# New tables of queue offsets for a fused attention and maxout kernel: own tables on both sides of a batch border, one operand turned by DMA there, casts of the first groups in load order

## The chip, the cores and the metric

One core of a Trainium2 chip. The metric is the device time of one execution in microseconds; times of several executions are given as the median. Each execution also has a span, the time from the first to the last instruction that the profile shows, mostly 1.8 us shorter than the timed figure (1.7 to 3.8 on record), and a mean granted TensorE clock (1.000 is full speed). All executions quoted are in the fast state. The engines are called PE (TensorE), DVE (VectorE), ACT (ScalarE), POOL (GpSimd) and SP (the engine that issues the DMAs).

## The reference, cut to what matters

```python
# q, k, v: (4, 12544, 128)   agents: (4, 49, 128)   w1, w2, w3: (128, 768)   w_out: (768, 128), all float32
def sm(a, b):
    s = scale * (a @ b.transpose(0, 2, 1))
    e = np.exp(s - s.max(-1, keepdims=True))
    return e / (e.sum(-1, keepdims=True) + 1e-09)
agent_v = sm(agents, k) @ v              # (4, 49, 128): needs all of k and v of a batch
x = (sm(q, agents) @ agent_v).reshape(B * S, D)
h = np.maximum(np.maximum(x @ w1, x @ w2), x @ w3)
return h @ w_out
```

Everything for q of batch b waits for the sums over all k and v of batch b. The kernel therefore reads k and v of batch b+1 while it works on q of batch b. A **batch border** is the place where the sums of the next batch are finished and q goes over to it.

## The kernel before

q is worked in 49 groups of 8 tiles of 128 rows (98 tiles a batch, so a border falls inside a group). For each group there are q scores and their exponential, six first-half products `u0..u5`, six relus of them (`a0..a5`, one in place), six second-half products `v0..v5`, six maxima (`x0..x5`, one of them a relu on ACT), 26 output matmuls for each of two output tiles, and two scalings. The instructions are not written in program order: each has an offset, and all are sorted by six units times the group plus the offset. The order of the sorted list is the order of each engine's queue; an instruction that waits at the head of a queue holds up what stands behind it, as the waits of 0.60 and 0.96 us in the prediction's timelines show.

```python
KEY = {"qt": -5.826, "qe": -4.714, "s": -3.397, "ex": -3.144, "ho": -2.653, ...}   # groups with k and v beside them
LATE = {"oc04": -102.316, "s": -5.143, "ex": -3.890, "ho": -3.007, ...}            # groups of the last batch
PRODUCT_KEYS = (-6.500, -6.260)
...
for op in sorted(ops, key=lambda o: o[:2]):     # in emit(): go, or wait for what it needs, or for a free tile
    if not go(op): late.append(op) ...
...
rings = {"uv": (3, []), "om": (2, []), "a": (3, [])}   # hidden tiles, small tiles, relu buffers
```

The work at a border is `k_tail`. A reduction on DVE sums the exponentials of k, a matmul with ones (the total) adds them over the partitions, a reciprocal and a multiplication give the normalised `avT`, and two products of it with the weights, evacuated by ACT, give the table `G` that the hidden products of the next batch use.

```python
def reduce():    nc.vector.tensor_reduce(out=d["e"], in_=Eacc[b]..., op=ALU.add)          # L328
def total():     nc.tensor.matmul(host[s][:, :A], ones, d["e"], ...)                      # L333
def normalise(): nc.vector.reciprocal(r, r) ; nc.vector.tensor_tensor(avT, Vacc, r, mult) # L339, L342
def product():   nc.tensor.matmul(...) ; nc.scalar.activation(G[b][:, c0:c1], src, Copy)  # L354, L361
...
elif s < SB:                                     # q of all groups but those of the last batch
    put("qt", turn_q, ring="om", frees=[("qe", s)])           # 8 PE transposes, L417
    put("qe", evacuate, ("qt", s), ...)                       # copy by DVE, L422
else:                                            # last batch
    at(key + K["s"] - 5.5, turn_q_dma, ("qe", s))             # DMA transpose
```

The softmax here doesn't subtract the row's maximum and nothing guards it: scores larger than these inputs give would overflow.

Of the kernel before, what the change touches and what calls it, by code (L numbers as in the profile page):

```python
# [16 lines left out]
def kernel(  # L17
# [32 lines left out]
    SB = (B - 1) * NT // GT  # L50
    assert NT % 2 == 0 and B * NT % GT == 0


    KEY = {
        "qt": -5.826, "qe": -4.714, "s": -3.397, "ex": -3.144, "ho": -2.653, "ks": -2.585,
        "ke": -1.395, "u0": -1.385, "u1": -0.945, "a0": -0.578, "a1": -0.505, "kv": -0.272,
        "sum": -0.189, "rec": -0.160, "ka": -0.096, "v0": -0.088, "u3": 0.041, "a3": 0.349,
        "x0": 0.448, "v1": 1.119, "v3": 1.156, "x1": 1.388, "u2": 1.556, "x3": 2.207, "u4": 2.461,
        "a2": 2.461, "v2": 2.540, "a4": 2.626, "x2": 2.904, "u5": 3.056, "v4": 3.065, "a5": 3.309,
        "x4": 3.802, "v5": 4.472, "x5": 5.223, "lin0": 6.482, "oc02": 6.840, "oc03": 7.560,  # L60
        "oc04": 8.286, "oc00": 8.460, "oc01": 8.460, "oc05": 8.461, "sc0": 8.860, "lin1": 9.007,
        "oc15": 9.269, "oc10": 9.504, "oc12": 9.761, "oc11": 11.129, "oc13": 11.301,
        "oc14": 11.651, "sc1": 11.652,
    }
    LATE = {
        "oc04": -102.316, "s": -5.143, "ex": -3.890, "ho": -3.007, "u0": -2.479, "sum": -2.401,
        "a0": -2.109, "u1": -1.115, "rec": -0.632, "u2": -0.631, "a1": -0.201, "v1": -0.150,
        "u3": 0.004, "a2": 0.202, "a3": 1.295, "x1": 1.296, "v0": 1.603, "v3": 1.692, "x0": 1.773,
        "v2": 1.787, "x3": 2.014, "x2": 2.121, "u4": 2.761, "u5": 2.826, "a4": 2.857, "v4": 3.484,
        "a5": 3.667, "v5": 3.891, "x4": 4.081, "x5": 4.963, "lin1": 6.405, "oc14": 6.642,  # L70
        "oc12": 6.780, "oc10": 8.128, "oc11": 8.220, "oc15": 8.227, "oc13": 8.498, "sc1": 8.670,
        "lin0": 9.304, "oc01": 9.553, "oc00": 9.686, "oc03": 11.369, "oc02": 11.426,
        "oc05": 11.684, "sc0": 12.804,
    }
    PRODUCT_KEYS = (-6.500, -6.260)

    const = ctx.enter_context(tc.tile_pool(name="const", bufs=1))
    loads = ctx.enter_context(tc.tile_pool(name="loads", bufs=14))
# [131 lines left out]
    def k_group(b, t0, n, key, s):  # L210

        d = {}
        early = s is None

        def load():
            for name, src in (("k", k), ("v", v)):
# [72 lines left out]
        if early:  # L289
            g = ("early", t0)  # L290
            at(key - 30, load)
            at(key - 5, cast_k)
            at(key - 4, cast_v)
            at(key, turn_k, ("kt", g), (), "uv", [("kt_out", g)])
            at(key + 0.5, evacuate, ("kt_out", g), [("kt", g)])

            last = [("normalise", 0)] if t0 + n == NT else []
            late = max(0, (key - last_key) / 6 + 2)
            at(min(key + 6.6, last_key + 0.58 + 0.02 * late), scores, ("ks", g), [("kt_out", g)],
               "uv", [("ka", g)] + last)  # L300
            at(min(key + 7, last_key + 0.64 + 0.01 * late), exps, ("ke", g), [("ks", g)])
            done = last_key + (0.6 + 0.1 * late if late >= 1 else 0.55)
            at(min(key + 13.2, done), values, ("kv", g), [("ke", g)])
            at(min(key + 13.6, done + 0.01), add_values, ("ka", g), [("kv", g)])
        else:
            at(key + KEY["ks"] - 22, load)
            at(max(key + KEY["ks"] - 10, last_key - 3.4), cast_k)
            at(max(key + KEY["ks"] - 8, last_key - 3.3), cast_v)
            if s > 1:
                at(max(key + KEY["ks"] - 6.5, last_key - 3.2), turn_k, ("kt_out", s))  # L310
            else:

                turn = 1.2 if s else last_key + 1.05
                at(turn, turn_k, ("kt", s), (), "uv", [("kt_out", s)])
                at(turn + 0.05, evacuate, ("kt_out", s), [("kt", s)])

            at(key + KEY["ks"] if s else KEY["u0"] + 0.6, scores, ("ks", s), [("kt_out", s), ("ho", s)])
            at(key + KEY["ke"], exps, ("ke", s), [("ks", s)])
            at(key + KEY["ke"] + 1.5, add_exps, ("kx", s), [("ke", s)])
            at(key + KEY["kv"], values, ("kv", s), [("ke", s)])  # L320
            at(key + KEY["ka"], add_values, ("ka", s), [("kv", s)])

    def k_tail(b, sum_key, keys, s):
        d = {}
# [60 lines left out]
    def q_group(s):  # L385
# [33 lines left out]
        def evacuate():  # L419
# [3 lines left out]
            else:  # L423
                nc.scalar.activation(d["qT"].rearrange("p j c -> p (j c)"), d["qT_ps"], AF.Copy)

        def turn_q_dma():
            d["qT"] = work.tile([P, GT, P], BF16, tag="qT", bufs=3, name="qT")
            nc.sync.dma_start_transpose(out=d["qT"], in_=d["qb"].rearrange("p j c -> p (j c)"))
# [83 lines left out]
            for src, r0, r1, m in rows(d["out"]):  # L512
                nc.sync.dma_start(out[r0:r1, :].rearrange("(p j) c -> p j c", j=m), src)

        K = KEY if s < SB else LATE
        new = [("product", tails[s], i) for i in range(2)] if s in tails else []

        def put(name, fn, *needs, ring=None, frees=()):
# [4 lines left out]
        if s == 0:  # L523
            at(last_key - 29.9, load)
            at(last_key - 3.5, cast)
            at(last_key + 0.82, turn_q, ("qt", 0), (), "om", [("qe", 0)])
            at(last_key + 0.825, evacuate, ("qe", 0), [("qt", 0)])
            at(last_key + 1, scores, ("s", 0), [("qe", 0)], "om", [("ex", 0)])
            at(last_key + 1.01, exps, ("ex", 0), [("s", 0)])
        elif s < SB:  # L530
            at(key + K["qt"] - 20, load)
            at(max(key + K["qt"] - 7, last_key - 3), cast)
            put("qt", turn_q, ring="om", frees=[("qe", s)])
            put("qe", evacuate, ("qt", s), *([("s", s - 3)] if s >= 3 else []))
        else:
            at(key + K["s"] - 24, load)
            at(key + K["s"] - 8, cast)
            at(key + K["s"] - 5.5, turn_q_dma, ("qe", s))
        if s:
            put("s", scores, ("qe", s), ring="om", frees=[("ex", s)])  # L540
            put("ex", exps, ("s", s), *old)
# [1 line left out]
        if s:  # L543
            put("ho", host_tile, ring="om", frees=[("rec", s)] + extra)
        else:
            at(KEY["u0"] - 0.04, host_tile, ("ho", 0), (), "om", [("rec", 0)] + extra)
        put("sum", sums, ("ex", s), ("ho", s),
            *([("ks", s)] if s in hosting else [("total", s)] if s + 1 in tails else []))
        put("rec", recips, ("sum", s))
# [12 lines left out]
        for o in range(2):  # L562
            put(f"lin{o}", lambda o=o: out_linear(o), ("ex", s), *new, ring="om", frees=[(f"sc{o}", s)])
            for f in range(NF):
                put(f"oc{o}{f}", lambda o=o, f=f: out_hidden(o, f), (f"lin{o}", s), (f"x{f}", s))
            put(f"sc{o}", lambda o=o: out_scale(o), ("rec", s),
                *[(f"oc{o}{f}", s) for f in range(NF)], *([("store", s - 3)] if s >= 3 else []))
        at(key + max(K["sc0"], K["sc1"]) + 0.5, store, ("store", s), [("sc0", s), ("sc1", s)])

    def ramp():  # L570

# [27 lines left out]
        if 4 <= g < len(first_sizes) - 5:  # L599
            fillers += [(first_key + 6.0 * g + 0.55, 3), (first_key + 6.0 * g + 1.3, 3)]  # L600
    k_tail(0, last_key, (last_key + 0.95, last_key + 1.02), None)
    for key, n in fillers + [(last_key + 0.9, 2), (last_key + 1.1, 2)]:
        at(key, lambda n=n: keep_busy(n), ("busy", key), (), "om", [("busy", key)])
    tails = {b * NT // GT: b for b in range(1, B)}
    hosting = set()
    for b in range(1, B):
        for g in range(NK):
# [2 lines left out]
            k_group(b, g * KT, min(KT, NT - g * KT), 6.0 * s, s)  # L610
    for s, b in tails.items():
        assert s - 1 not in hosting
        k_tail(b, 6.0 * (s - 1) + KEY["ho"] + 0.001, [6.0 * s + PRODUCT_KEYS[i] for i in range(2)], s - 1)
    for s in range(NQ):
        q_group(s)
    ramp()
# [33 lines left out]
```

## Time and profile before

| | |
|---|---|
| time | 470.73 us, median of 3 (470.11 to 471.0) |
| span of the profiled execution | 467.5 us, clock 0.998 |
| PE, DVE, ACT busy | 94%, 87%, 85% |
| ordinary group / group ahead of a border / late group | 8.35 / 10.85 / 7.84 us |

Four groups of the page's costliest instructions carry the argument. The columns are line, engine, operation, output and input, count, then busy us and mean ns of one, then the idle time ahead of them and what ended most of it.

```profile
L485 DVE TENSOR_TENSOR r<-uv_ps,a_sb 128x1024 bf16<-128x1024 f32 x245 | 297.3, 1220 | 13.9 <-PE uv_ps L460 4.2
L475 ACT ACTIVATE a_sb<-uv_ps 128x1024 bf16<-128x1024 f32 x245 | 241.3, 1028 | 11.5 <-PE uv_ps L460 11.1
L460 PE MATMUL uv_ps<-e_q,G 49*128 49x512 bf16 (+3 forms) x1248 | 185.5, 368 | 4.8 <-DVE r L485 2.9
...
L490 PE MATMUL o_ps<-G,e_q 128*128 128x256 bf16 x196 | 38.0, 276 | 1.8 <-DVE o_sb L506 1.8
```

L485 is the maximum, L475 the relu, L460 the hidden products, L490 the first matmuls of an output tile and L506 the scaling that frees one. PE waited 4.8 us ahead of hidden products and 1.8 us ahead of output tiles in the whole run. A group of L460 or L485 mixes all stages, so the stages are read from windows and timelines.

In all that follows the row-sum matmuls of a group are its marker. "c10 to c14" is the time from those of group 10 to those of group 14, counted from 0: the four groups around the first border.

### The profile page before, as it was taken

The numbers are of one execution on the slowest core, as the hardware profiler recorded it, in microseconds if no ns is written. First come the engines' busy times: TensorE is split into PE (matmuls) and PEld (weight loads), VectorE is DVE, ScalarE is ACT, GpSimd is POOL, SyncE is SP. The second block draws the span as 40 slices with busy tenths as digits, with TensorE's granted clock in tenths as the row PEclk, the third lists the DMA queues.
The fourth block names the chain that finished last, engine by engine and source line by source line (L and its number), as shares of the span: only waits on it lengthen the run. The fifth ranks groups of instructions, "written<-read, shape, count | busy, mean of one in ns | idle before, by whom it ended". The sixth has DMA issues, their size and how long they took to land.

```text
span 467.5 us, 13338 instructions
## 1 busy us (share of the span) xinstructions
PE 437.3 (94%) x5478; PEld 273.4 (58%) x5478; DVE 408.3 (87%) x519; ACT 396.7 (85%) x461; POOL 165.8 (35%) x166
## 2 busy tenths in 40 slices
PE   2398899999999999999989999999989999999996
PEld 2376366666655666666656666666655555555554
DVE  3155699999998999999998999999988999999995
ACT  3267889989898899898989898998989999999992
POOL 3244863644460545535262446353220111010000
PEclk9999999999999999999999999999999999999999
DMA  8999999998987999987986999976365776553512
GB/s 324 397 411 405 408 289 361 315 325 215 328 277 260 285 263 328 304 266 234 314 291 225 286 335 285 275 226 192 126 114 158 215 169 183 150 145 100 105 77 105
DMA packets 79464, 117.75 MB, mean 252 GB/s; under 512 B 53223, under 2 KB 54699, under 8 KB 79403
## 3 DMA queue, kind: packets, MB, share of 16 engines
q1 hardware_dynamic: 79200, 116.80, 81.8%
q8 instruction: 42, 0.69, 0.6%
q14 instruction: 19, 0.16, 0.1%
q10 hardware_dynamic: 203, 0.10, 0.1%
HBM read 78.74 MB, written 25.69 MB: 223 GB/s over the span
## 4 chain that ended last, share of the span: by engine, by line
PE 78%; DMA 10%; DVE 6%; ACT 3%; issue 1%; POOL 0%; SPq 0%; DVEq 0%; ACTq 0%; POOLq 0%
PE uv_ps L460 33%; PE o_ps L499 28%; DMA st<-in_k_dram 7%; PE o_ps L490 6%; DVE r L485 4%; PE m_ps L417 4%; PE m_ps L434 3%; DMA wst<-in_moe_w_dram 2%; ACT a_sb L475 2%; PE m_ps L266 1%; PE m_ps L255 1%; DVE o_sb L506 1%; DMA ag_st<-in_agents_dram 1%; PE m_ps L448 1%; PE uv_ps L354 1%
## 5 line engine op out<-in xcount | busy, mean ns | idle before, releaser
L485 DVE TENSOR_TENSOR r<-uv_ps,a_sb 128x1024 bf16<-128x1024 f32 x245 | 297.3, 1220 | 13.9 <-PE uv_ps L460 4.2
L475 ACT ACTIVATE a_sb<-uv_ps 128x1024 bf16<-128x1024 f32 x245 | 241.3, 1028 | 11.5 <-PE uv_ps L460 11.1
L460 PE MATMUL uv_ps<-e_q,G 49*128 49x512 bf16 (+3 forms) x1248 | 185.5, 368 | 4.8 <-DVE r L485 2.9
L499 PE MATMUL o_ps<-wo_bf,r 128*128 128x128 bf16 x2352 | 176.4, 220 | 0.0
L499 PEld LDWEIGHTS <-r 128*128 128x128 bf16 x2352 | 137.6, 98 | 44.2 <-issue 42.7
L460 PEld LDWEIGHTS <-G 49*128 49x128 bf16 x1248 | 56.1, 93 | 66.3 <-issue 31.9
L283 POOL TENSOR_TENSOR Eacc<-Eacc,e_k 128x441 f32<-128x441 f32 (+1 forms) x30 | 30.5, 1015 | 130.5 <-ACT e_k L260 130.5
L506 DVE TENSOR_TENSOR o_sb<-o_ps,recips 128x512 f32<-128x512 f32 x98 | 67.6, 690 | 9.7 <-PE o_ps L499 6.8
L412 POOL CAST q_bf<-st 128x1024 bf16<-128x1024 f32 x49 | 51.0, 1040 | 70.6 <-DMA qT<-q_bf 68.8
L483 ACT ACTIVATE r<-uv_ps 128x1024 bf16<-128x1024 f32 x49 | 50.1, 1023 | 26.3 <-PE uv_ps L460 26.3
L223 POOL CAST k_bf<-st 128x1152 bf16<-128x1152 f32 (+2 forms) x45 | 50.4, 1119 | 28.9 <-DMA st<-in_k_dram 26.1
L472 ACT ACTIVATE uv_ps<-uv_ps 128x1024 f32<-128x1024 f32 x49 | 49.6, 1013 | 0.3 <-PE uv_ps L460 0.2
L490 PE MATMUL o_ps<-G,e_q 128*128 128x256 bf16 x196 | 38.0, 276 | 1.8 <-DVE o_sb L506 1.8
L230 POOL CAST v_bf<-st 128x1152 bf16<-128x1152 f32 (+1 forms) x33 | 37.5, 1135 | 0.5 <-DMA st<-in_v_dram 0.5
L440 ACT ACTIVATE e_q<-m_ps 128x512 bf16<-128x512 f32 x49 | 29.9, 610 | 0.5 <-PE m_ps L434 0.5
L243 DVE COPY kT<-uv_ps 128x1152 bf16<-128x1152 bf16 (+1 forms) x14 | 9.9, 709 | 17.9 <-PE uv_ps L237 17.7
L228 ACT ACTIVATE v_bf<-st 128x1152 bf16<-128x1152 f32 (+1 forms) x12 | 12.9, 1072 | 14.6 <-DMA st<-in_v_dram 14.6
L490 PEld LDWEIGHTS <-e_q 128*128 128x128 bf16 x196 | 12.8, 97 | 20.6 <-issue 20.6
L417 PEld LDWEIGHTS <-q_bf 128*128 128x128 bf16 x288 | 16.2, 98 | 14.8 <-issue 13.2
L422 DVE COPY qT<-m_ps 128x1024 bf16<-128x1024 bf16 x35 | 23.8, 681 | 0.0
L417 PE MATMUL m_ps<-ident,q_bf 128*128 128x128 bf16 x288 | 22.2, 220 | 0.8 <-POOL q_bf L412 0.8
L237 PE MATMUL uv_ps<-ident,k_bf 128*128 128x128 bf16 x116 | 11.7, 262 | 10.8 <-POOL k_bf L223 10.8
(68 smaller groups left out, 234.7 us busy)
## 6 DMA issues: line engine op xcount, KB each, us to landing
st<-in_q_dram SPq DMA_DIRECT2D x46, 512.0 KB, 4.6
out_dram<-o_sb SPq DMA_DIRECT2D x46, 512.0 KB, 3.5
st<-in_k_dram SPq DMA_DIRECT2D x40, 576.0 KB, 6.6
st<-in_v_dram SPq DMA_DIRECT2D x40, 576.0 KB, 7.4
st<-in_k_dram SPq DMA_DIRECT2D x3, 512.0 KB, 6.3
st<-in_v_dram SPq DMA_DIRECT2D x3, 512.0 KB, 7.1
wst<-in_moe_w_dram SPq DMA_DIRECT2D x3, 384.0 KB, 10.4
st<-in_q_dram SPq DMA_DIRECT2D x2, 384.0 KB, 4.2
```

The costliest lines, as they stand in the source:

```text
L223: nc.gpsimd.tensor_copy(out=d["kb"][:, :n, :], in_=d["k"][:, :n, :])
L230: nc.gpsimd.tensor_copy(out=d["vb"][:, :n, :], in_=d["v"][:, :n, :])
L412: nc.gpsimd.tensor_copy(out=d["qb"], in_=d["q"])
L417: nc.tensor.transpose(t[:, j * P:(j + 1) * P], d["qb"][:, j, :], ident)
L460: nc.tensor.matmul(t[:, h, j0 * P:j1 * P], G[b][h * H:h * H + A, col + f * P:col + (f + 1) * P], d["e"][h * H:h * H + A, j0 * P:j1 * P], s ...
L472: nc.scalar.activation(u, u, AF.Relu)
L475: nc.scalar.activation(a_sb[f], u, AF.Relu)
L483: nc.scalar.activation(r, v_ps[f], AF.Relu)
L485: nc.vector.tensor_tensor(out=r, in0=v_ps[f], in1=a_sb[f], op=ALU.max)
L490: nc.tensor.matmul(t[:, i * 2 * C:(i + 1) * 2 * C], d["e"][:, jj * P:(jj + 1) * P], G[batch[jj]][:, C1O:C1O + 2 * C], start=(i == 0), stop ...
L499: nc.tensor.matmul(t[:, c:c + C], r_sb[f][:, h, jj * P:(jj + 1) * P], wo_bf[:, f, :], start=False, stop=True, skip_group_check=True)
L506: nc.vector.tensor_tensor(out=d["out"][:, j:j + m, :], in0=d["o", o].rearrange("p (j c) -> p j c", c=C), in1=d["r"][:, j:j + m].unsqueeze( ...
```

## The change

Its intent, as far as the diff shows it: remove the waits at the borders and in the late groups by giving the queues a better order. Five things change.

- Every table is tuned anew, and two are added: `BORDER` for the group ahead of a border and `BEGIN` for the first mixed group behind it.
- q of the groups ahead of a border is turned by DMA, no longer by PE and DVE.
- The border's two products move: the first 2.2 units earlier, the second 4.4 units later.
- At the start, POOL casts q and k of the first groups in the order of their loads. Two filler matmuls are added.
- Loads, stores and casts get fixed offsets of their own.

```diff
+    tails = {b * NT // GT: b for b in range(1, B)}
     KEY = {
-        "qt": -5.826, "qe": -4.714, "s": -3.397, "ex": -3.144, "ho": -2.653, "ks": -2.585,
+        "qt": -5.778, "qe": -4.748, "s": -2.658, "ex": -2.602, "ho": -2.097, "ks": -1.591,
         ... (all offsets anew)
     LATE = {
-        "oc04": -102.316, "s": -5.143, "ex": -3.890, "ho": -3.007, "u0": -2.479, "sum": -2.401,
+        "s": -4.972, "ex": -4.712, "ho": -2.917, "u0": -1.818, "sum": -1.767, "a0": -1.468,
         ... (all offsets anew)
-    PRODUCT_KEYS = (-6.500, -6.260)
+    BORDER = { "oc05": -40.989, ..., "s": -5.570, "ex": -4.719, "ho": -4.600, "sum": -2.514, ... }
+    BEGIN = { "sc0": -46.305, ..., "qt": -5.396, "qe": -4.152, "s": -2.593, "ex": -2.139, ... }
+    PRODUCT_KEYS = (-8.717, -1.818)
+    def table(s):
+        if s + 1 in tails:
+            return BORDER
+        return BEGIN if s in tails and s < SB else KEY if s < SB else LATE
 ... in k_group
-            at(max(key + KEY["ks"] - 10, last_key - 3.4), cast_k)
+            at(max(key - 12.6, last_key - 3.4 + 0.2 * s), cast_k, ("k_cast", s))
 ... in q_group
+        q_dma = s >= SB or s + 1 in tails
-        elif s < SB:
-            at(max(key + K["qt"] - 7, last_key - 3), cast)
+        elif not q_dma:
+            at(max(key - 12.8, last_key - 3.45 + 0.2 * s), cast, ("q_cast", s))
         else:
-            at(key + K["s"] - 8, cast)
-            at(key + K["s"] - 5.5, turn_q_dma, ("qe", s))
+            at(key - 14.3, cast)
+            at(key - 12.3, turn_q_dma, ("qe", s))
 ...
-    for key, n in fillers + [(last_key + 0.9, 2), (last_key + 1.1, 2)]:
+    for key, n in fillers + [(last_key + 0.9, 2), (last_key + 1.1, 2), (KEY["u1"] + 0.61, 2)]:
```

## The prediction

> **What bounds the kernel now.** I read the page first, then the chain of waits, then windows by stage, then the timeline of one border, and last the listing of both programs' instructions by engine.
>
> ```profile
> PE 437.3 (94%) x5478; PEld 273.4 (58%) x5478; DVE 408.3 (87%) x519; ACT 396.7 (85%) x461; POOL 165.8 (35%) x166
> PEclk9999999999999999999999999999999999999999
> ```
>
> Three engines are over 85% busy, and the clock is full throughout. No engine has much room, so time can only come from stretches where the engines hold each other up. The windows show where those are. I cut them at the four small row-sum matmuls (L448) that open each group of 8 token tiles.
>
> ```profile
> 66.65:125.12 58.47, 58.47 (x763) 37.26 (x759) 56.08 (x72) 53.40 (x64) 27.98 (x28) 1.00 1.04 306
> 133.45:144.30 10.85, 9.29 (x109) 5.33 (x105) 9.64 (x16) 8.96 (x10) 6.15 (x6) 1.00 0.73 236
> 144.30:152.74 8.44, 8.40 (x116) 5.39 (x115) 7.70 (x10) 7.71 (x11) 1.16 (x2) 1.00 0.88 288
> 380.40:451.00 70.60, 70.32 (x741) 38.71 (x739) 65.98 (x73) 65.62 (x73) 6.24 (x6) 1.00 0.51 137
> ```
>
> The columns are length, then PE, weight loads, DVE, ACT and POOL busy, clock, DMA share, GB/s. Seven ordinary groups take 58.47 us, so 8.35 us each, with PE never empty. The group before a batch border takes 10.85 us with PE busy only 9.29. The nine late groups (no k or v left to read) take 70.60, so 7.84 each. The same cuts give the whole ledger: 48.3 us up to the first row sums, 10.0 for the first group, 9 ordinary groups 75.2, the first border with its two mixed groups and the next (four groups) 36.0, ordinary 66.8, second border 36.0, ordinary 67.1, third border (two groups) 17.5, twelve late groups 94.2, and 16.5 to drain: 467.5 in all. The timed median is 470.73.
>
> Four ordinary groups would be 33.4, so each border costs 2.6 us more than that. The timeline of the border group says why (PE, then DVE):
>
> ```profile
> 137.69 0.41 PE L434 MATMUL m_ps<-qT,agT 128*64 128x512 bf16 x2
> 138.69 0.38 PE L490 MATMUL o_ps<-G,e_q 128*128 128x256 bf16 x2 [0.60 <-DVE o_sb L506]
> ...
> 140.53 0.61 PE L460 MATMUL uv_ps<-e_q,G 49*128 49x512 bf16 x4
> 142.10 0.39 PE L460 MATMUL uv_ps<-e_q,G 49*128 49x512 bf16 x2 [0.96 <-DVE r L485]
> ```
> ```profile
> 137.10 0.95 DVE L328 TENSOR_REDUCE e_sum<-Eacc 128x49 f32<-128x441 f32 x1
> 137.96 0.68 DVE L506 TENSOR_TENSOR o_sb<-o_ps,recips 128x512 f32<-128x512 f32 x1
> ...
> 140.19 0.48 DVE L339 RECIPROCAL m_ps<-m_ps 128x49 f32<-128x49 f32 x1 [0.42 <-PE m_ps L333]
> ```
>
> The reduction of the softmax sums (L328) stands in the DVE queue ahead of the scaling that frees an output tile (L506), and PE waits 0.60 for that tile. Later the reciprocal (L339) heads the DVE queue waiting for PE's total, the maxima behind it come late, and PE waits 0.96 for a maximum to free a hidden tile. Block starts put the two PE losses at 0.67 and 1.11 us, 1.78 together.
>
> **What the Trainium skill says.** "Perfetto Trace Analysis", Identifying the Most-Contended Engine, says that matmul busy time does not tell how close one is to the limit. The trace agrees: ordinary groups show PE at 58.47 of 58.47, yet within a group the blocks of matmuls start up to 0.16 us later than equal blocks elsewhere. "TensorE: Matmul & The Clock Gate", Back-to-back issue gap, gives N/2.4 + 2.5 ns, 55.8 ns for 128 columns; here transposes in a row start 56 ns apart, so eight of them take PE 0.45 us although one record lasts 220 ns. "DMA: Bandwidth & Descriptors", DMA Transpose (X-bar), allows the DMA transpose of 2-byte data from SP or ACT; all here come from SP, and q already lands that way in a median 4.4 us, 13 times. "PSUM — Partial Sum Buffer", Specifications, gives 8 banks of 2 KiB; the kernel's tiles (3 of two banks, 2 of one) fill them all. No run shows the count, but the two waits above are waits for tiles, so the order of the queues is what can be changed.
>
> **The change part by part.**
>
> 1. Ordinary groups. The table of offsets is new, but in the listing groups 2 to 9, and those far from a border later, have the same order on PE, DVE and ACT as before. An offset has no effect beyond the order. Change: 0 on 25 or so groups.
>
> 2. q by DMA ahead of a border (groups 11, 23, 35). Each drops 8 PE transposes (0.45 us), one DVE copy (0.68 us long, next start 0.60 later) and adds a DMA transpose of 4.4 us in a stretch where DMA is at 0.73. It is issued some 12 offset units ahead (6 units are one group, so about 17 us), so I expect no wait for it.
>
> 3. The borders. The sum over a border's four groups, by PE blocks: the rows cost 36.0 now, of which 2.5 are losses (1.78 above, the rest small), so 33.5 of work; less 0.45 gives 33.05. But losses do not vanish. I went through the new queues by hand with durations from the trace (maximum 1.22, next one 1.13 later; ACT pass 1.02, next 0.92 later; 0.43 to 0.5 from a matmul's start to its reader). The reduction now comes first in the border group (1.65 us after the sums it is done), the query scores and their exponential come early, and the total must wait for the tile that the exponential frees: PE loses about 0.5 there. The maxima then run behind by the reduction and the reciprocal, and PE waits another 0.3 for a tile at the second-half products. In the next group PE waits about 0.6 for ACT, which must first evacuate the new product (1.03) in the middle of its passes. By these starts the 20-matmul block of the second group begins 12.0 us after the border group's sums, where the trace has 13.4. But the second product, formerly in the border group, now stands after that block and costs 0.5. That leaves 0.9 per border, 1.8 for two.
>
> 4. The third border goes likewise, without transposes in the next group: two groups 17.5 now, by the same steps 16.2. About 0.2 of output work slides to the next group. Gain 1.1.
>
> 5. Late groups. Old order on ACT: exponential, 5 relus, in-place relu (L472), final relu (L483) with 0.54 idle before it. New order: the exponential between those two. That looks like 0.54 saved in each of 12, but the final relu still cannot start before 0.54 after the end of L472, and PE's next first-half product waits for the tile that it frees. The loop from that product round to itself is 0.43 to ACT, 0.92 to the second relu, 1.03 for it, 0.1 to PE, 0.50 to DVE, 1.22 maximum, 0.09 to the fifth relu (which takes the buffer that maximum frees), 0.92 to L472, 1.02 for it, 0.54, 1.02 for the final relu, 0.03 to PE: 7.82, which is the 7.83 measured, and every link is still there. Gain 0 to 0.05 a group; I take 0.2 for all.
>
> 6. The start. POOL now casts q of group 1 before k of group 1, as they are loaded; before, the queue stood 1.52 us idle for k's load with q's cast behind it, and PE waited 0.53 for q. A relu moves ahead of an exponential (1.00 idle before that now). Against it, two filler matmuls (0.43) and k's transposes come earlier. Up to the first sums the load from HBM sets the time, unchanged. Gain 0.5.
>
> Sum: 0 + 1.8 + 1.1 + 0.2 + 0.5 = 3.6 us, so 467.1.
>
> **The rivals.**
>
> A. The borders gain all they could: 2.6 each for three, plus 1 at the start and 0.54 for each late group (6.5). That is 15 us, 455. For it speaks that the orders were evidently retuned there; against it the loop of step 5, which closes at 7.82 whichever way ACT is ordered, and the tiles in step 3.
>
> B. A new wait takes the place of the old. The two groups at a border now hold the reduction, reciprocal and both products in other places; were the new losses 2 us rather than 1.4 per border, the gain would be nil: 470. Early query scores also need the DMA transpose earlier; if it were late, PE would stand still in the border group. The DMA share of 0.73 speaks against.
>
> C. The bound in late groups is throughput and not that loop: ACT at 65.62 of 70.60, PE blocks without loss 7.43 of 7.83. Then the ACT reorder would give up to 0.3 a group, 3.6 more, and the time would be about 463.5. The ACT idle of exactly 0.54 in each group speaks for it, the loop against.
>
> D. The loads bound the first 170 us (DMA busy tenths 8 and 9), and a quicker start is handed back as a wait for k or q. No such wait shows after 57 us before; it would take 0.5 from my sum.
>
> **Range and chances.** B and D push to 470, C to 463.5; A I hold for out of reach. I take 467.1, with 464.5 to 469.3 for 8 in 10. Two per cent faster is 461.3, which needs A or most of it: 0.03. Slower by 2% needs a stall of 13 us nowhere in sight: 0.01. Within 2%: 0.96.
>
> **What would show each step.** Ordinary groups still 8.35 apart (1). No wait on qT<-q_bf by PE (2). The border group and next together about 18.4 us rather than 19.3 from sums to sums, with losses on PE at the total and before the new product's first use, and none behind L328 (3, 4). Late groups at 7.8; if 7.5, C was right (5). First to second row sums 9.5 rather than 10.0 (6). I am wrong above all if late groups move, or if the mixed groups after a border, whose queues I followed only halfway, come out of step and pay back more than 0.5.

## The result and the profile after

| | before | changed |
|---|---|---|
| time, median of 4 | 470.42 us (469.88 to 471.0) | 466.69 us (465.91 to 467.3) |
| ratio | | 0.992, 95% interval 0.9897 to 0.9942: the same within 2% |
| span of the profiled execution | 467.5 us | 465.3 us |

A ratio here is the mean time of one kernel's fast runs over that of the other's of the same rounds, so it is not quite the ratio of the medians. The outputs are correct. In the changed kernel's profile the line numbers are higher: hidden products L492, output matmuls L531 and L522, scores L466, maximum L517, scaling L538, relus L507, L504 and L515, exponential L472, reduction L357, reciprocal L368, product L383, casts L252 and L441.

From the changed kernel's page, the busy times and the clock:

```profile
PE 436.1 (94%) x5452; PEld 274.3 (59%) x5456; DVE 405.6 (87%) x516; ACT 396.6 (85%) x461; POOL 166.6 (36%) x166
PEclk9999999999999999999999999999999999999999
```

PE, DVE and ACT are no busier than before; POOL is by 0.8 us and the weight loads by 0.9. Then its windows, columns as in the prediction: seven ordinary groups, the border group, the next group, and nine late groups.

```profile
67.24:125.69 58.45, 58.45 (x764) 37.25 (x760) 56.05 (x72) 53.41 (x64) 28.00 (x28) 1.00 1.03 305
134.01:139.85 5.84, 5.33 (x61) 3.12 (x57) 5.80 (x12) 4.94 (x6) 5.84 (x6) 1.00 0.80 234
139.85:152.32 12.47, 12.41 (x156) 7.59 (x155) 11.02 (x13) 11.60 (x15) 1.33 (x3) 1.00 0.84 284
377.24:448.37 71.13, 70.43 (x741) 39.72 (x739) 65.72 (x73) 65.99 (x73) 5.21 (x5) 1.00 0.46 126
```

Ordinary groups are unchanged at 8.35. The border group and the next together take 18.31 where they took 19.29, and PE is empty for 0.57 of that where it was empty for 1.60. (The row sums now come at another place in the border group, so only the pair can be compared.) The nine late groups take 71.13 where they took 70.60: they became **slower**.

The timeline of PE at the same border, with the instructions that carry the change:

```profile
134.75 0.41 PE L466 MATMUL m_ps<-qT,agT 128*64 128x512 bf16 x2
...
136.46 0.42 PE L362 MATMUL m_ps<-e_sum,ones 128*128 128x49 f32 x2 [0.44 <-ACT e_q L472]
...
139.29 0.62 PE L383 MATMUL uv_ps<-wall,avT 128*64 128x512 bf16 x6
```

and of DVE:

```profile
134.80 0.95 DVE L357 TENSOR_REDUCE e_sum<-Eacc 128x49 f32<-128x441 f32 x1
135.66 1.22 DVE L517 TENSOR_TENSOR r<-uv_ps,a_sb 128x1024 bf16<-128x1024 f32 x1
136.92 0.48 DVE L368 RECIPROCAL m_ps<-m_ps 128x49 f32<-128x49 f32 x1
```

The scores now come 0.74 us after the sums (they came 4.24 after), the reduction is the first long work of DVE, and PE waits 0.44 for the tile that the exponential frees, ahead of the total. The two waits that the prediction showed, 0.60 and 0.96, are gone.

The ledger of both profiled executions, from the starts of the row sums, with the prediction's part beside it (us):

| stage | before | changed | difference | predicted |
|---|---|---|---|---|
| to the cast of the first q | 41.91 | 42.88 | +0.97 | 0 |
| from there to c1 | 16.39 | 16.02 | -0.38 | -0.5 |
| c1 to c10, ordinary | 75.15 | 75.12 | -0.03 | 0 |
| c10 to c14, first border | 36.01 | 34.97 | -1.04 | -0.9 |
| c14 to c22, ordinary | 66.80 | 67.07 | +0.26 | 0 |
| c22 to c26, second border | 36.01 | 34.97 | -1.05 | -0.9 |
| c26 to c34, ordinary | 67.08 | 66.78 | -0.31 | 0 |
| c34 to c36, third border | 17.48 | 15.93 | -1.54 | -1.3 |
| c36 to c48, late | 94.18 | 94.65 | +0.47 | 0.0 |
| c48 to the last scaling | 12.83 | 13.36 | +0.53 | 0 |
| last store | 3.71 | 3.61 | -0.10 | 0 |
| span | 467.55 | 465.33 | -2.21 | -3.6 |

(The prediction's 1.1 at the third border is 1.3 less 0.2 of work that slides into the late groups; that 0.2 and its 0.2 of gain there cancel.) The first row isn't the change's: up to that cast the loads set the time, and in 12 other traced executions of kernels of both kinds it comes at 41.9 to 42.6. Without it the sum is -3.2. The +0.26 and -0.31 are single groups, longer by 0.28 in one place of each execution, in both kernels and in different groups; no run here explains them. Among executions at a clock of 1.000, the kernel before has a mean span of 467.78 (29 of them) and the changed kernel 464.5 (one), so -3.3. All of this fits the timed ratio.

### The profile page after: what moved, and what is told of

It is laid out like the page before. It is cut to its first block, busy times and chain, and to the rows that moved or that the text cites. A ratio compares the mean times of both kernels' runs of the same rounds, so it can differ in the third digit from the quotient of the medians.

```text
span 465.3 us, 13301 instructions
## 1 busy us (share of the span) xinstructions
PE 436.1 (94%) x5452; PEld 274.3 (59%) x5456; DVE 405.6 (87%) x516; ACT 396.6 (85%) x461; POOL 166.6 (36%) x166
## 4 chain that ended last, share of the span: by engine, by line
PE 77%; ACT 6%; issue 3%; DVE 3%; ACTq 0%; DVEq 0%
PE uv_ps L492 33%; PE o_ps L531 28%; PE o_ps L522 5%; ACT a_sb L507 4%; PE m_ps L446 4%; PE m_ps L466 3%; DVE r L517 2%; PE m_ps L295 2%; PE m_ps L284 1%; PE m_ps L480 1%; ACT uv_ps L504 1%; ACT e_q L472 1%; PE uv_ps L383 1%; PE o_ps L613 0%; ACT G L390 0%
## 5 line engine op out<-in xcount | busy, mean ns | idle before, releaser
L517 DVE TENSOR_TENSOR r<-uv_ps,a_sb 128x1024 bf16<-128x1024 f32 x245 | 297.4, 1220 | 15.6 <-PE uv_ps L492 5.9
L507 ACT ACTIVATE a_sb<-uv_ps 128x1024 bf16<-128x1024 f32 x245 | 240.6, 1027 | 13.2 <-PE uv_ps L492 11.7
L492 PE MATMUL uv_ps<-e_q,G 49*128 49x512 bf16 (+3 forms) x1248 | 186.3, 368 | 2.2 <-DVE r L517 0.6
L531 PE MATMUL o_ps<-wo_bf,r 128*128 128x128 bf16 x2352 | 174.7, 220 | 0.2 <-DVE r L517 0.2
L531 PEld LDWEIGHTS <-r 128*128 128x128 bf16 x2352 | 137.8, 98 | 39.8 <-issue 37.9
L492 PEld LDWEIGHTS <-G 49*128 49x128 bf16 x1248 | 57.9, 93 | 63.4 <-issue 31.1
L538 DVE TENSOR_TENSOR o_sb<-o_ps,recips 128x512 f32<-128x512 f32 x98 | 67.5, 689 | 9.4 <-PE o_ps L531 6.5
L441 POOL CAST q_bf<-st 128x1024 bf16<-128x1024 f32 x49 | 51.0, 1043 | 63.1 <-DMA qT<-q_bf 61.8
L515 ACT ACTIVATE r<-uv_ps 128x1024 bf16<-128x1024 f32 x49 | 50.2, 1024 | 21.8 <-PE uv_ps L492 21.7
L252 POOL CAST k_bf<-st 128x1152 bf16<-128x1152 f32 (+2 forms) x45 | 51.0, 1132 | 28.8 <-DMA st<-in_k_dram 27.1
L504 ACT ACTIVATE uv_ps<-uv_ps 128x1024 f32<-128x1024 f32 x49 | 49.5, 1011 | 1.0 <-ACT a_sb L507 0.7
L522 PE MATMUL o_ps<-G,e_q 128*128 128x256 bf16 x196 | 38.0, 276 | 0.0
L472 ACT ACTIVATE e_q<-m_ps 128x512 bf16<-128x512 f32 x49 | 29.8, 609 | 0.5 <-PE m_ps L466 0.5
L522 PEld LDWEIGHTS <-e_q 128*128 128x128 bf16 x196 | 12.5, 97 | 18.5 <-issue 17.8
L446 PEld LDWEIGHTS <-q_bf 128*128 128x128 bf16 x264 | 14.8, 98 | 13.1 <-issue 11.5
L451 DVE COPY qT<-m_ps 128x1024 bf16<-128x1024 bf16 x32 | 21.8, 680 | 0.0
L446 PE MATMUL m_ps<-ident,q_bf 128*128 128x128 bf16 x264 | 20.4, 220 | 0.3 <-POOL q_bf L441 0.3
## 6 DMA issues: line engine op xcount, KB each, us to landing
wst<-in_moe_w_dram SPq DMA_DIRECT2D x3, 384.0 KB, 10.8
```

What stands on the lines that cost most here:

```text
L252: nc.gpsimd.tensor_copy(out=d["kb"][:, :n, :], in_=d["k"][:, :n, :])
L441: nc.gpsimd.tensor_copy(out=d["qb"], in_=d["q"])
L446: nc.tensor.transpose(t[:, j * P:(j + 1) * P], d["qb"][:, j, :], ident)
L492: nc.tensor.matmul(t[:, h, j0 * P:j1 * P], G[b][h * H:h * H + A, col + f * P:col + (f + 1) * P], d["e"][h * H:h * H + A, j0 * P:j1 * P], s ...
L504: nc.scalar.activation(u, u, AF.Relu)
L507: nc.scalar.activation(a_sb[f], u, AF.Relu)
```

## The experiments

Twelve kernels ran, all with correct outputs, each in five rounds against the kernel before on the same chip. Medians of before in the three sessions were 469.73, 470.05 and 469.97 us.

### The tables at the border taken away

```diff
-        if s + 1 in tails:
-            return BORDER
-        return BEGIN if s in tails and s < SB else KEY if s < SB else LATE
+        return KEY if s < SB else LATE
-    PRODUCT_KEYS = (-8.717, -1.818)
+    PRODUCT_KEYS = (-6.500, -6.260)
-        q_dma = s >= SB or s + 1 in tails
+        q_dma = s >= SB
```

> The changed kernel with the borders undone: no own tables beside a border, q ahead of it turned by PE again, old product offsets; start and late table as changed. Theory (the gain is made at the borders, 1.04 us at each of two and 1.54 at the third in the traces): about 470.3, that is 3.6 us slower than the changed kernel, with the group before a border back at 10.85 us and no change of ordinary groups. Rival (the gain comes from the new start and the new tables elsewhere): within 1 us of the changed kernel's 466.7.

Measured: 477.47 us, ratio 1.016 (1.0145 to 1.0175). Both expectations missed. The edit doesn't give the old border back. The new ordinary table, used at a border, puts four output matmuls, not eight, ahead of the first product, and the products come out of step. In its PE timeline of the first border (line numbers are two lower than in the changed kernel: L490 is a hidden product, L381 the new product):

```profile
141.67 0.39 PE L490 MATMUL uv_ps<-e_q,G 49*128 49x512 bf16 x2 [0.96 <-DVE r L515]
142.79 0.63 PE L381 MATMUL uv_ps<-wall,avT 128*64 128x512 bf16 x6 [0.41 <-DVE r L515]
144.53 0.52 PE L381 MATMUL uv_ps<-wall,avT 128*64 128x512 bf16 x4 [0.56 <-ACT G L388]
```

c10 to c14 takes 38.08, 2.1 more than in the kernel before. The third border takes 20.97 for 17.48; in the profiled execution the granted clock was 0.5 from 353.8 to 360.6 us, inside it. So the retuned ordinary table with the old product offsets serves a border worse than the old table did, but this run doesn't say what the border tables are worth. Three of the next four experiments are built from the kernel before for that reason.

### The reduction early, alone, in the kernel before

```diff
-            at(sum_key - 1, reduce, ("sum_e", b), [("kx", s - 1)])
+            at(sum_key - 3.05, reduce, ("sum_e", b), [("kx", s - 1)])
```

> The kernel before with one thing moved: the reduction of the softmax sums goes to the head of the DVE queue of the border group, two maxima and a copy earlier, as in the changed kernel; all else stays, PE turns q. Theory (the reduction in front of the scaling costs PE 0.60 at each border by its queue place): the wait of 0.60 for the output tile goes, 0.3 to 0.6 us per border, time 0.9 to 1.8 below the kernel before. Rival (the 0.86 that the reduction takes on DVE is handed on to the maxima behind it wherever it stands): border groups still 10.8, time unchanged.

Measured: 470.73 us, ratio 1.0011 (1.0002 to 1.002), so slower by about 0.5. The rival, which said 10.8 a border group and no change, held in the main. From its PE timeline:

```profile
136.77 0.39 PE L460 MATMUL uv_ps<-e_q,G 49*128 49x512 bf16 x2 [0.59 <-DVE r L485]
...
142.71 0.39 PE L460 MATMUL uv_ps<-e_q,G 49*128 49x512 bf16 x2 [0.96 <-DVE r L485]
```

The wait of 0.60 for an output tile is gone, and one of 0.59 for a hidden tile stands two blocks earlier. The 0.86 that the reduction holds DVE is only moved ahead of other work that PE needs. The border group takes 11.06 rather than 10.85; three times 0.21 is 0.63, and the spans at clock 1.000 differ by 0.63 (468.41 against 467.78).

### q by DMA alone, in the kernel before

```diff
-        elif s < SB:
+        elif s < SB and s + 1 not in tails:
 ...
         else:
-            at(key + K["s"] - 24, load)
-            at(key + K["s"] - 8, cast)
-            at(key + K["s"] - 5.5, turn_q_dma, ("qe", s))
+            at(key - 32, load)
+            at(key - 14.3, cast)
+            at(key - 12.3, turn_q_dma, ("qe", s))
```

> The kernel before, with q of the three groups ahead of a border turned by DMA (cast and transpose issued as in the changed kernel) and nothing else changed. It takes 8 PE transposes (0.44 us) and one copy on VectorE (0.60) out of each border group; the order of the rest stays. Theory (this removal is the core of the border's gain): the border group falls from 10.85 to 10.2 or less, the first and second border's four groups from 36.0 to 35.4 or less, the time by 1.5 to 2.5: 467.6 to 468.6. Rival (the gain is in the order of the new tables; work taken away here only turns into longer waits behind the reduction and the reciprocal): border group 10.6 or more, time 469.3 or more.

Measured: 468.06 us, ratio 0.9958 (0.9945 to 0.9972). The border group takes 10.42, between the two expectations, and c10 to c14 35.57; the time lies in the theory's range. The gain is 0.44 at each of the three borders, the size of PE's eight transposes; three times that is 1.3, and the rest of the 1.9 between the medians is not at the borders. The copy of 0.60 that DVE no longer makes gives nothing more, which the block starts explain: the block with the wait of 0.60 became 0.59 shorter, but the hidden products ahead of it became 0.45 longer and those behind it 0.16 longer. From its PE timeline, the first of these two:

```profile
135.52 0.61 PE L460 MATMUL uv_ps<-e_q,G 49*128 49x512 bf16 x4 [0.28 <-ACT uv_ps L472]
```

PE, now early, waits for ACT's in-place relu instead. Less work for DVE alone doesn't pay here, because ACT has become what PE waits for.

### q by DMA and the reduction early, in the kernel before

The two edits above together.

> The same, and the reduction also ahead of the border group's maxima. Alone, the early reduction lost 0.2 a border, because the first maxima came 0.86 later and PE waited 0.6 for one. With the copy of q (0.60) gone from the same stretch of the VectorE queue, theory: that wait shrinks to 0.0 to 0.3, and the 0.60 behind the reduction is gone too: border group 9.9 or less, a border 35.0 or less, like the changed kernel; time 466.2 to 467.3. Rival (waits come back wherever the reduction stands): border group 10.2 or more, time no better than with the DMA alone.

Measured: 469.89 us, ratio 1.0002 (0.9991 to 1.0013): a clear miss for the theory. The rival's two lines both held. The border group takes 11.04. From its PE timeline:

```profile
136.46 0.39 PE L460 MATMUL uv_ps<-e_q,G 49*128 49x512 bf16 x2 [0.28 <-ACT uv_ps L472]
137.42 0.39 PE L460 MATMUL uv_ps<-e_q,G 49*128 49x512 bf16 x2 [0.57 <-DVE r L485]
```

Both waits are there, one for ACT and one for the maximum that the reduction pushed back. An early reduction, in the old order of everything else, costs 0.63 a border with q by DMA and 0.21 without. (Its profiled execution has a dip of the clock at the start, so its span isn't used; the border lies later.)

### The changed kernel with q ahead of a border turned by PE again

```diff
-        ..., "x4": -21.066, "s": -5.570, ...
+        ..., "x4": -21.066, "qt": -5.850, "qe": -5.600, "s": -5.570, ...
-        q_dma = s >= SB or s + 1 in tails
+        q_dma = s >= SB
```

> The changed kernel with q ahead of a border turned by PE again, transposes and copy placed just ahead of the early scores. Theory (the early scores need the DMA): PE waits for the copy of q (0.43 from transposes to it, 0.68 for it, 0.1 back, less what can be put between), so each border grows by the 0.44 of transposes and about 1.0 of wait: 1.2 to 1.8 each, time 469.9 to 472, no better than the kernel before. Rival (the transposes are hidden work, the order of the tables is what gains): 0.3 to 0.6 each, 467.4 to 468.5.

Measured: 470.33 us, ratio 1.0007 (0.9997 to 1.0016). The border group and the next take 19.28, against 18.31 in the changed kernel and 19.29 before. That is 0.97 more than the change, between the theory's 1.2 and the rival's 0.6, and the time lies in the theory's range. The PE timeline names the wait:

```profile
134.42 0.61 PE L446 MATMUL m_ps<-ident,q_bf 128*128 128x128 bf16 x8
135.80 0.41 PE L466 MATMUL m_ps<-qT,agT 128*64 128x512 bf16 x2 [0.78 <-DVE qT L451]
```

The early scores stand 0.78 for DVE's copy of q. (Where I put the transposes wasn't tuned; another place may cost less.) With the DMA-only run this makes a square:

| us | tables of before | tables of the change |
|---|---|---|
| c10 to c14, q by PE | 36.01 | 35.94 |
| c10 to c14, q by DMA | 35.57 | 34.97 |
| c34 to c36, q by PE | 17.48 | 16.90 |
| c34 to c36, q by DMA | 17.04 | 15.93 |

At the first border DMA alone is worth 0.44, the tables alone 0.07, and both 1.04. At the second (c22 to c26) the tables alone cost 0.28 (36.29), DMA alone and both are as at the first. Each makes the other pay: the tables put the scores first, and only the DMA makes them ready that early. The two border tables and the product offsets were always kept or taken away together, so what each of them is worth stays open.

### Two product blocks exchanged in the ordinary groups

```diff
-        "ke": -1.172, "u0": -0.804, "u1": -0.767, ...
+        "ke": -1.172, "u0": -0.825, "u1": -0.767, ...
```

> The changed kernel with one offset moved in the ordinary table: on PE the first product of the next group goes ahead of the last second-half product of this one. ACT idles 0.18 in each ordinary group before the relu of that product (it starts 0.42 after the product, and the product stands behind the other by 0.22). Theory (the loop of an ordinary group runs through that relu): up to 0.18 less per ordinary group, 8.17, 4.9 us for 27. Rival (the product put back makes the last maximum, the scaling and PE's turn of q that waits for its tile later by as much): 8.35 or more, time 467 to 469.

This puts the first first-half product of a group ahead of the last second-half product of the group before; the listing shows the same forms in the same order, with other tiles. Measured: 469.8 us, ratio 0.999 (0.9976 to 1.0003), 3 us slower than the changed kernel. Its ordinary groups take 8.51 rather than 8.35. In its ACT timeline of one group:

```profile
94.81 1.02 ACT L515 ACTIVATE r<-uv_ps 128x1024 bf16<-128x1024 f32 x1 [0.76 <-PE uv_ps L492]
```

The 0.18 of idle is gone, as the theory said, but the final relu waits 0.76 where it waits 0.54 in the changed kernel, and PE's block of four hidden products ahead of its turn of q takes 0.73 rather than 0.54: the rival's direction, and a time outside both expectations. Each of the three stretches of eight or nine such groups costs 1.3 us; these 3.9 are somewhat more than the 3 us that the times show. So exchanging one pair of short blocks costs nearly all that the change won; other exchanges were not tried.

### Late groups: ACT's old order

```diff
     LATE:
-        "ex": -4.712, ... "rec": -0.824
+        "ex": -3.950, ... "rec": -0.600
```

> The changed kernel with two offsets of the late table moved, so that ACT and DVE have their old order there (exponential after the final relu; reciprocal of the row sums after the sixth maximum); PE's order stays new. Theory (a loop through PE, ACT and DVE sets a late group, and the place of the exponential is not in it): late groups 7.83 to 7.86, time within 0.5 us of the changed kernel. Rival (ACT's 0.54 us of idle per late group was the bound and the new order removes it): late groups 0.5 longer than the changed kernel's, time 472.

Measured: 466.53 us, ratio 0.9929 (0.9916 to 0.9941), late groups 7.83 to 7.86: the theory held. ACT's order is as before the change, yet the late groups stay at the change's 7.86. This also rules out the prediction's rival C, by which ACT's order was worth 3.6 us.

### Late groups: four relu buffers

```diff
-        rings = {"uv": (3, []), "om": (2, []), "a": (3, [])}
+        rings = {"uv": (3, []), "om": (2, []), "a": (4, [])}
-                a_sb[f] = work.tile([P, 2, 512], BF16, tag="a_sb", bufs=3, name="a_sb")
+                a_sb[f] = work.tile([P, 2, 512], BF16, tag="a_sb", bufs=4, name="a_sb")
```

In the changed kernel:

> The changed kernel with 4 buffers instead of 3 for the relu's output (a_sb); the order on every engine stays as it is. Theory: in a late group one link of the loop is the fifth relu waiting for the maximum that frees its buffer; without it the loop is 0.43 + 5 x 0.92 + 1.56 + 1.07 = 7.66, so late groups go from 7.86 to about 7.66 and the time to 464.5; ordinary groups (8.35), whose chain has no such link, stay. Rival (late groups are bound by the throughput of an engine, or by PSUM tiles alone): no change, 466.7.

Measured: 466.24 us, ratio 0.9923 (0.9911 to 0.9936), late groups 7.862, unchanged. A miss: the buffer isn't the link that binds there. With the edit of ACT's old order on top:

> The changed kernel with ACT and DVE in their old order in the late groups (as in late_ex_rec) and 4 relu buffers (as in r4_after). Theory, as corrected after these two: the changed kernel's late groups have two loops of nearly one length, 7.85: one through the fifth relu waiting for its buffer, one through the exponential, which must come between in-place and final relu but gets its scores late. late_ex_rec opened the second, r4_after the first, and each left the other. With both open what remains is first-half product, relu, relu, L472, final relu, next product, maximum: 0.43+0.92+0.91+1.56+1.07+1.11+0.50+1.28 = 7.78, so late groups 7.78 and the time 0.9 us below the changed kernel. Rival (the throughput of PE or a third loop holds 7.85): no change against late_ex_rec.

Measured: 466.72 us, ratio 0.993 (0.9909 to 0.9952), late groups 7.863. Again no movement. ACT's timelines show where its idle time went. First the kernel before, one late group:

```profile
416.56 1.02 ACT L483 ACTIVATE r<-uv_ps 128x1024 bf16<-128x1024 f32 x1 [0.54 <-PE uv_ps L460]
417.48 0.59 ACT L440 ACTIVATE e_q<-m_ps 128x512 bf16<-128x512 f32 x1
418.04 4.90 ACT L475 ACTIVATE a_sb<-uv_ps 128x1024 bf16<-128x1024 f32 x5
```

then the changed kernel:

```profile
421.29 0.60 ACT L472 ACTIVATE e_q<-m_ps 128x512 bf16<-128x512 f32 x1
421.89 1.02 ACT L515 ACTIVATE r<-uv_ps 128x1024 bf16<-128x1024 f32 x1
423.39 1.94 ACT L507 ACTIVATE a_sb<-uv_ps 128x1024 bf16<-128x1024 f32 x2 [0.47 <-PE uv_ps L492]
```

In each late group ACT twice hands a tile to PE and needs PE's answer: from the in-place relu to the final relu, and from the final relu, which frees a tile, to the next relu. The exponential can cover one of the two trips. Before, it covered the second and 0.54 stood open at the first. The change puts it at the first, and 0.47 stands open at the second. ACT idles nearly as long either way.

This is not what binds in the changed kernel. From the run with ACT's old order to the one with four buffers on top, the in-place relu comes 0.06 earlier after the sums, the wait of the final relu grows from 0.55 to 0.60, and PE's hidden products keep their places within 0.01. A loop that fits all three runs goes through PE and DVE alone. In the changed kernel (PE, then DVE):

```profile
418.33 0.62 PE L531 MATMUL o_ps<-wo_bf,r 128*128 128x128 bf16 x8
...
421.18 0.82 PE L492 MATMUL uv_ps<-e_q,G 49*128 49x512 bf16 x6
...
424.09 0.77 PE L492 MATMUL uv_ps<-e_q,G 49*128 49x512 bf16 x4
```
```profile
416.73 1.23 DVE L517 TENSOR_TENSOR r<-uv_ps,a_sb 128x1024 bf16<-128x1024 f32 x1
...
421.68 2.35 DVE L517 TENSOR_TENSOR r<-uv_ps,a_sb 128x1024 bf16<-128x1024 f32 x2 [0.22 <-PE uv_ps L492]
...
424.59 1.22 DVE L517 TENSOR_TENSOR r<-uv_ps,a_sb 128x1024 bf16<-128x1024 f32 x1
```

The maximum of 416.73 frees a tile, and PE takes it at 418.01, 1.28 after the maximum began. From there PE goes from block to block without a wait for 3.17, to the product of 421.18. The maximum that reads it starts 0.50 later; two maxima take 2.35; PE takes the freed tile 0.06 later, at 424.09; and the maximum of that product starts after another 0.50. The sum is 7.86, one group. With the old order of PE the same sum is 7.79, as the run with four buffers in the kernel before shows (below). No run opened this loop alone, so it is read from the traces and not shown by an experiment.

### Late groups: the old late table from group 37 on

```diff
+    OLD = { (the LATE table of the kernel before) }
-        return BEGIN if s in tails and s < SB else KEY if s < SB else LATE
+        return BEGIN if s in tails and s < SB else KEY if s < SB else LATE if s < 37 else OLD
```

> The changed kernel with the old late table for groups 37 to 48. From the sums of group 36 to the end the trace of the kernel before took 110.7 us and that of the changed kernel 111.6. Theory (the new late table is no gain, its order costs a little): late groups back to 7.83, stretch to the end shorter by 0.3 to 0.9 us unless the three groups of transition cost more; time 466.0. Rival (the new table gains, and the 0.9 comes from the state in which the border leaves the engines): late groups or drain longer than the changed kernel's, time 467 or more.

Measured: 467.5 us, ratio 0.9948 (0.9929 to 0.9967). From group 40 on the groups take 7.834, as in the kernel before: so the 0.027 a group belongs to the new late table. But as the tables change over, the steps from c36 on take 7.32, 9.30, 8.47 and 8.18, and c36 to the last scaling takes 109.1, against 108.0 in the changed kernel and 107.0 before. So the theory was right on the group and the rival on the time: exchanging the table in the middle cost more than it gave.

### The start: k of group 1 cast ahead of its q, as before

```diff
-            at(max(key - 12.6, last_key - 3.4 + 0.2 * s), cast_k, ("k_cast", s))
+            at(max(key - 12.6, last_key - 3.4 + 0.2 * s) - (0.076 if s == 1 else 0), cast_k, ("k_cast", s))
```

> The changed kernel with one cast put back: POOL casts k of group 1 before q of group 1, everything else as changed. Theory (q's cast stood behind a cast that waits for a later load): PE's turn of q in the first group waits about 0.9 us more for POOL, the second row sums come 0.3 to 0.6 us later than the landing of the loads allows, time 467.1. Rival (the load from HBM alone sets the start): within 0.2 us of the changed kernel, with the distance from q's first cast to the second row sums still 16.0 us.

Measured: 466.58 us, ratio 0.9927 (0.9914 to 0.9941), no slower than the changed kernel. The profiled execution was slower (span 466.1, the others 464.2 to 465.1), and the excess lies ahead of c1: from the first cast of q to c1 it took 17.7 us, for 16.0 in the changed kernel. Its windows show why; the last three columns are the granted clock, the DMA share and GB/s.

```profile
49.00:50.00 1.00, 0.79 (x9) 0.26 (x7) 0.23 (x3) 0.33 (x2) 1.00 (x3) 1.00 1.03 414
...
51.00:52.00 1.00, 1.00 (x11) 0.87 (x9) 0.18 (x1) 0.00 (x0) 1.00 (x2) 0.50 0.99 394
52.00:53.00 1.00, 1.00 (x6) 0.13 (x4) 0.93 (x2) 0.00 (x0) 1.00 (x2) 0.50 1.04 414
```

The clock was halved. Over 48 to 58 us its mean is 0.83, so a halved clock for 10 x 0.17 / 0.5 = 3.4 us. The Trainium skill, "TensorE: Matmul & The Clock Gate", Part 1: The HAM clock gate (the "warmup" mystery), says that the array runs at half its clock after an idle window of some 3.4 us until a busy one has passed, and that the windows don't start with the kernel; the length agrees, and that another execution of the same kernel escapes fits too. What counts as idle is another matter (see the last section). A traced execution of the DMA-and-reduction kernel has the same dip at the same place. The start therefore differs by a microsecond or more between executions of one kernel, and what the cast order is worth stays open; the time is the rival's. In executions without a dip the step from the first cast of q to c1 takes 16.0 in the changed order (eight traces) and 16.3 to 16.4 in the old one (three): the start as a whole is worth 0.3 to 0.4.

### Two edits in the kernel before: four relu buffers, and q of group 1 cast early

```diff
-        rings = {"uv": (3, []), "om": (2, []), "a": (3, [])}
+        rings = {"uv": (3, []), "om": (2, []), "a": (4, [])}
-            at(max(key + K["qt"] - 7, last_key - 3), cast)
+            at(max(key + K["qt"] - 7, last_key - (3.45 if s == 1 else 3)), cast)
```

> The kernel before with two edits that touch different stages: four relu buffers, not three (late groups), and the cast of group 1's q ahead of that of its k (start). Late groups: the prediction's loop passes through a relu that waits for a buffer; if that binds, they fall from 7.83 to between 7.55 and 7.75. Rival: ScalarE's own queue with the one round trip of 0.54 to PE closes the loop without that buffer, as the changed kernel's did not move either: 7.83. Start: theory, first to second row sums fall from 10.0 to between 9.4 and 9.7; rival (the loads decide) 9.9 or more. Time by the theories 467 to 468.5; by both rivals 470.

Measured: 474.02 us, ratio 1.0089 (1.0061 to 1.0117). The second edit was badly made: it put the cast of group 1's q ahead of the casts of group 0's k and v too. From its POOL timeline:

```profile
46.23 1.04 POOL L412 CAST q_bf<-st 128x1024 bf16<-128x1024 f32 x1 [3.08 <-DMA st<-in_q_dram]
47.22 1.15 POOL L223 CAST k_bf<-st 128x1152 bf16<-128x1152 f32 x1
```

POOL stood 3.08 us for a load while k, which had been cast at 43.42 in the kernel before, waited behind. The clock fell to 0.63 to 0.94 in the windows between 36 and 58 us, and c1 came 4.3 us later. It says nothing on the change's start, but it shows what an order against the loads costs. The late groups of this run are clean: 7.793 rather than 7.834, so both expectations missed. The buffer did bind before, but only by 0.04. Behind it stands the loop of PE and DVE, which sums to 7.79 here (1.27 + 3.17 + 0.44 + 2.35 + 0.05 + 0.51, in the order given above); ACT's open trip only grew, to 0.59:

```profile
428.41 1.02 ACT L483 ACTIVATE r<-uv_ps 128x1024 bf16<-128x1024 f32 x1 [0.59 <-PE uv_ps L460]
```

No experiment beat the changed kernel beyond the noise; four buffers in it gave 466.24, inside its own range.

## Why the prediction was right or wrong

The class, the time (467.1 for a measured 466.69) and the range held. By its steps:

1. **Ordinary groups.** Right: 8.350 after, 8.353 before. The exchange of two blocks shows that this was not to be taken for granted.
2. **q by DMA.** Right that nothing waits for it: no wait on it by PE shows at a border, at a DMA share of 0.80 to 0.84. The step counted 0.45 of PE for it, and alone it gives 0.44. It did not see that the tables depend on it, worth another 0.5 a border.
3. **First two borders.** Right in the main, slightly small: 1.04 for 0.9 each. PE waits 0.44 at the total, for 0.5; the block of 20 begins 11.88 after the sums, for 12.0; the pair of groups takes 18.31, for 18.4. The step's other two waits, 0.3 for a tile and 0.6 for ACT, don't show as waits: PE is empty for 0.57 in the whole pair, that 0.44 included. Its two ways of counting a border don't meet either: 33.05 of work and 1.4 of losses make 34.45, its block starts make 35.1, and the trace has 34.97. The step expected the waits to be paid back in part, and the kernels with the early reduction show that happening.
4. **Third border.** Right in direction: 1.54 for 1.3 ahead of c36.
5. **Late groups. This step failed.** "Gain 0 to 0.05 a group; I take 0.2 for all" is the term mis-sized: the late groups and the tail cost 1.0, not gained 0.2. Its finding that the old idle of 0.54 was no gain to be had was right. Wrong was "every link is still there". Its loop through the relu buffer binds before the change, by only 0.04 (7.793 with a fourth buffer), and in the changed kernel not at all. By the traces a second loop, through PE and DVE alone, sets 7.86 there; the step did not count it, and in the old order it lay hidden at 7.79. The old table in the new kernel gives 7.834 back, so the new table costs 0.027 a group, 0.3 in 12. Why the new order makes that loop longer, mostly 0.50 rather than 0.44 from a product's start to its maximum, stays open. The rest of the 0.47 and the 0.53 behind c48 are measured, but not taken apart.
6. **The start.** 0.38 for 0.5, confirmed by the traces without a clock dip. The measure proposed for it, 9.5 from first to second sums, was a bad one: that interval is 8.88, because c0 itself comes 0.74 later after the cast.

The three borders gave 0.5 more than predicted, and the late part and the start 1.1 less; half of the error cancels, so that the total was this close is partly luck. Of the rivals, B did not occur in the change, but it did in both kernels with the early reduction. (Its sum is off: 0.6 more of loss would have left 0.3 of the 0.9 a border, not nothing.) C is refuted by the run with ACT's old order, D found nothing: the changed kernel's page puts 0.3 us of PE's idle time down to casts of q in the whole run, where that of the kernel before has 0.8.

## What to carry to other kernels

Where three engines hand tiles round in fixed queues, an instruction moved out of one wait's way can land in front of another, as the early reduction and the late exponential did here: ask for each move what the instruction had been covering where it stood. An idle stretch on one engine need not be in the loop that binds: add up the loop before choosing the edit. Three edits on ACT's side left the late groups at 7.86. Two parts of a change can be worth little apart and much together, so undo each alone as well as the whole before crediting one of them. A table tuned for a steady state may need tables for its edges (without them this kernel took 477.47), and a partial return to the old one is not an undo.

## What the Trainium skill lacked or had wrong

- "TensorE: Matmul & The Clock Gate", HAM oscillation, gives as its rule of thumb that PE should have no idle gap over some 3.4 us. The two executions with a halved clock at the start had no such gap: the longest stretch without a matmul in the 10 us ahead of the dip was 1.0 us (0.7 in the other, 0.9 if transposes count as idle). Nor had the one at the third border of the kernel without border tables (1.0). In the 3.4 us ahead of each of these dips PE was busy for 1.9 to 2.3. So the page's length of 3.4 us fits, but the rule of thumb doesn't cover these; its next section, on a second failure mode, reports such oscillation from frequent short idle times, without a figure for how much is too much. Other executions with the same gaps kept the full clock.
- "TensorEngine Tiling (Array Packing)", Key Properties, says that changing the tiling mode drains the array, but no page that I read gives the cost. Here four output matmuls take 319 ns from their start to a following hidden product (49 of the array's 128 rows), but 233 ns to a following matmul of the full array; two hidden products take 216 ns more inside a block, and about 105 ns are added when the block ends. So each change between the two kinds costs some 0.1 us. That it is this drain was not tested.
